# Lead stage of a decay-attention and two-layer MLP kernel: score and bonus matmuls over 128 keys, dummy matmuls of 512 columns, two groups of dummies more

## The chip, the cores and the metric

The kernel runs on one core of a Trainium2 chip. The metric is the device time of one execution in microseconds (us), and less is better. A core has five engines with a queue of instructions each: TensorE (PE in the rows, its weight loads PEld), VectorE (DVE), ScalarE (ACT), GpSimd (POOL) and SyncE (SP), which here issues the DMAs. An engine works through its queue in order; between engines, semaphores make one wait for another's result.

## The reference

An attention with a decaying state for 4 batches, 8 heads, 768 steps and 48 dimensions per head, and behind it two layers with a hidden width of 2048 over the 3072 tokens of width 384.

```python
for t in range(S):
    cur = einsum('bhd,bhe->bhde', u * k_t, v_t)           # the bonus: this step's own key and value
    y[:, :, t] = einsum('bhd,bhde->bhe', r_t, state + cur)
    state = w * state + einsum('bhd,bhe->bhde', k_t, v_t)  # w decays the state
x = y as 3072 x 384
x = relu(x @ moe_w_in) ** 2 @ moe_w_out
h = x @ moe2_w_in;  out = (h - tanh(h)) @ moe2_w_out
```

## The kernel before

**Tiling.** The 768 steps are cut into 6 chunks of 128 (`C`), so there are 24 tiles of 128 tokens (`NTAU`), four (`TPB`) for each block of 512 tokens (`TB`); block 0 holds the first chunk of all four batches. The two layers work on 6 blocks with 16 column groups of the hidden width each. Their matmuls are 128x512 in fp32r, with two-part operands, so that one column group takes 9 matmuls into the hidden layer and 9 out of it.

**The lead stage.** The first chunk of each batch has no state before it. So tiles 0 to 3 are done by functions of their own, `lead_*`, and this is what the change touches. For tile i: `lead_prod` (DVE) multiplies r and k for the bonus; `lead_k` and `lead_r` (DVE) put the decay into k and r; `lead_sums` (PE, L567, tile `pk`) sums the product over the dimensions, weighted with u, and gives one number for each key and head; `lead_bt` (ACT, L578) copies these to SBUF, `lead_diag` (POOL, L351) sets them on the diagonal of a score tile `am`; `lead_turn` (PE, L574) transposes k, `lead_kn` (ACT, L584) copies that out; `lead_b` (PE, L602, tile `sc`) computes the scores of 4 heads, `lead_m` (DVE, L613) copies them into `am` below the diagonal; `lead_c` (PE, L636, tile `y`) multiplies the scores with the values; `lead_cs` and `lead_st` (PE L650, ACT L668) compute the state; `lead_eh` and `lead_el` (ACT L659, DVE L663) give the block's input `xt` for the first layer. Besides, `table_keys` (DVE, L281, tile `kh`) and `table_turn` (PE, L291) make a table of decays that later tiles use.

**fp32 and array tiles.** These small matmuls are in plain fp32, and the trace shows each as two records, with two weight loads; a transpose has one. A matmul is given a part of the 128x128 array by where its operands lie: r and k of the two heads of a pair lie on partitions 0 to 47 and 64 to 111, and the keys of a tile are cut into two halves `c` of 64 (`L`), so the four matmuls of a head pair in `lead_b` take the four quarters of the array.

**Dummies.** `fill(n)` issues n bf16 matmuls with zero weights into a bank whose result nobody reads. 28 (`WARM`) stand ahead of everything, and `fl` in the order below issues 4 more at a time.

**Order.** The order on every engine is written out by hand in `first_order`, a list of names with an index, from which `make` calls the functions; `pb` is `lead_sums`, `tp` `lead_turn`, `lb` `lead_b` (two of them for each tile), `lm` `lead_m`, `lc` `lead_cs`, `ly` `lead_c`, `lst` `lead_st`, `tt` `table_turn`, `fl` `fill`, `h` a column group of the first layer, `c0` to `c3` the steps that unpack a weight tile `raw` (`c1a` is DVE's L96). From `h.0` on the blocks of the two layers follow each other to the end.

Of the kernel before, what the change touches and what calls it, by code (L numbers as in the profile page):

```python
# [8 lines left out]
BF16 = mybir.dt.bfloat16  # L9
# [16 lines left out]
def decay_attention_moe_moe_kernel(  # L26
# [10 lines left out]
    nc = tc.nc  # L37
    NTAU, _, _, NP, C = rk.shape
# [3 lines left out]
    GP = 64 + D  # L42
# [3 lines left out]
    TB = 512  # L46
    NB = NT // TB
    TPB = TB // C
    WARM = 28

    wts = ctx.enter_context(tc.tile_pool(name="wts", bufs=1))
    ident = wts.tile([128, 128], F32, name="ident")
    zero = wts.tile([GP, 128], BF16, name="zero")
# [10 lines left out]
    def bank(i, name):  # L64
        return ps.tile([128, 512], F32, tag=f"bank{i}", name=name)
# [7 lines left out]
    def load_w(layer, f):  # L73
        raw = cv.tile([128, 2 * DM, 2], U32, tag="raw", name="raw", bufs=5)
        nc.sync.dma_start(
            out=raw.rearrange("p x two -> p (x two)"), in_=(w1 if layer == 1 else w2).bitcast(U32)[f]
        )
        raw_t[layer, f] = raw
# [60 lines left out]
    L = C // 2  # L139
# [10 lines left out]
    low = ac.tile([128, 128], F32, name="low")  # L150
    ub = ac.tile([128, GPS], F32, name="ub")
# [3 lines left out]
    tk = tr[:, :, 127::-1]  # L155
# [8 lines left out]
    ucol = wu[:, NP:3 * NP].rearrange("p (P a) -> p P a", a=2)  # L164
# [9 lines left out]
    def hold():  # L174
        nc.gpsimd.tensor_copy(turn[0:made[0].shape[0]], made[0])

    rk_t = {}
# [11 lines left out]
    pr_t = {}  # L189
# [78 lines left out]
    def side():  # L268
        if not side_t:
            side_t.append(bank(2, "pt"))  # L270
        return side_t[0]
# [7 lines left out]
    def table_keys():  # L279
        kh = gp.tile([GP, NP, L], F32, tag="g", name="kh")  # L280
        nc.vector.tensor_tensor(  # L281
            kh, pw[:, 0, :, 63::-1], pw[:, 0, :, 32:33].to_broadcast([GP, NP, L]), op=ALU.mult,
        )
        kh_t.append(kh)

    def table_turn():
        kh_t.append(side())
        for p in range(NP):
            for a in range(2):
                q = slice(64 * a, 64 * a + D)  # L290
                nc.tensor.matmul(  # L291
                    kh_t[1][half(a), p * D:(p + 1) * D], lhsT=kh_t[0][q, p, :], rhs=ident[q, q],
                    start=True, stop=True,
                )

    def table_nat():
        nc.scalar.activation(out=kt_tab, in_=kh_t[1][:, 0:GPS], func=AF.Copy)

    def fill(n):
        for q in range(n):  # L300
            nc.tensor.matmul(
                side()[:, 256:512], lhsT=zero, rhs=low[0:GP].bitcast(BF16), start=True, stop=True
            )

    def setup_pool():
# [40 lines left out]
    def half(a):  # L346
        return slice(64 * (1 - a), 64 * (2 - a))
# [215 lines left out]
    def lead_sums(i):  # L563
        pk = pk_t[i] = bank(1, "pk")
        for p in range(NP):
            for c in range(2):
                nc.tensor.matmul(  # L567
                    pk[64 * c:64 * c + 64, NP * GP + 2 * p:NP * GP + 2 * p + 2],
                    lhsT=pr_t[i][:, p, c * L:(c + 1) * L], rhs=ucol[:, p, :], start=True, stop=True,
                )  # L570

    def lead_turn(i):
        for p in range(NP):
# [20 lines left out]
    def lead_b(d):  # L594
        i, e = divmod(d, 2)
        b0 = 3 if d % 2 else 5
        sc0[d] = sc = [bank(b0 + a, "sc") for a in range(2)]
        for z in range(2):
            for a in range(2):
                s = slice(64 * a, 64 * a + D)  # L600
                for c in range(2):
                    nc.tensor.matmul(  # L602
                        sc[a][64 * c:64 * c + 64, z * C:(z + 1) * C],
                        lhsT=rk_t[i][s, 1, 2 * e + z, c * L:(c + 1) * L], rhs=rk_t[i][s, 0, 2 * e + z, :],
                        start=True, stop=True,
                    )

    am_b = []

# [12 lines left out]
    def lead_z():  # L622
        for d in range(4):
            am_b.append(gp.tile([128, 4, C], F32, tag="ghi", name="am", bufs=4))
# [270 lines left out]
    for j in range(1, NB - 1):  # L895
        for f, o in visit.items():
            i = TPB * (j + 1) + o
# [19 lines left out]
    def front(n):  # L917
# [4 lines left out]
            act2_flush()  # L922

    first_order = """
        pr.0 k.0 fl.2 fl.0 r.0 pb.0 tp.0 rk.1 rk.2 pr.2 k.2 v.1 v.0 fl.1 tk.0 gt.5 kn.0 tt.0 pr.1 v.2 tn.0 r.1 k.1
        ub.0 lbt.0 lb.0 lb.1 pb.1 lbt.1 w.0 c1a.0 dg.0 lm.0 tp.1 lc.0 rk.3 lm.1 lb.2 dg.1 lm.2 kn.1 lst.0 ly.0 r.2
        lc.1 v.3 lst.1 lb.3 pr.3 k.3 pb.2 lm.3 lb.4 lx.0 lxl.0 lbt.2 dg.2 r.3 gt.19 c0.0 tp.2 kn.2 pb.3 lc.2 w.2 c0.2
        w.1 lbt.3 c0.1 ly.1 lx.1 dg.3 gt.3 lb.5 L.4 nu.4 c1b.0 c2.0 c1a.1 lm.4 lm.5 tp.3 lxl.1 lb.6 lm.6 w.4 w.3 lb.7
        lm.7 L.5 c3.0 kn.3 c1b.1 lst.2 lc.3 ly.2 ly.3 lst.3 fl.3 lx.2 lxl.2 lx.3 lxl.3 h.0 nr.4 c1a.2 c2.1 c1b.2 c0.4
        c3.1 h.1 c1a.4 rl.0 c2.2 c3.2 sq.0 w.5 w.7 w.6 c1a.3 c0.3 c1b.3 hi.0 rl.1 gt.14 sq.1 hi.1 c2.3 c1b.4 c0.5 ar.5  # L930
        rd.5 lo.0 h.2 rl.2 sq.2 gt.4 c3.3 g2.0 g2.1 g2l.0 gt.1 w.8 c1a.5 c1b.5 h.3 ar.4 rd.4 c2.4 c3.4 w.9 h.4 hi.2
        lo.1 lo.2 c2.5 c3.5 g2.2 c1a.6 c1a.8 c0.7 rl.3 h.5 sq.3 hi.3 lo.3 c0.6 w.10 c1a.7 gt.2 c1b.7 g2.3 gt.10 ak.4
        ns.4 c1b.6 nk.4 c0.8 c1b.8 rl.4 sq.4 hi.4 g2l.2 g2.4 g2l.1 c2.7 c2.6 c3.7 rl.5 c3.6 nu.5 b.4 gt.6 c2.8 lo.4
        sq.5 c1a.10 hi.5 lo.5 c0.10 gt.9 nr.5 d.4 c3.8 gt.11 s0p.4 gt.18 sv.4 L.6 s1a.4 s1d.4 c1a.9 c0.9 c1b.10 ns.5
        ak.5 gt.8 w.12 h.7 h.6 rl.6 rl.7 sq.6 w.11 w.13 g2l.3 g2.5 hi.6 sq.7 hi.7 c1b.9 c2.9 nu.6 h.8 g2l.4 m.4 g2.6
        lo.6 lo.7 g2.7 g2l.5 g2l.6 c2.10 c0.11 c3.9 h.9 nk.5 c1a.11 rl.8 nr.6 c1b.11 sv.5 gt.0 sq.8 w.14 ns.6 s1p.4
        s1a.5 nk.6 d.5 ak.6 s0p.6 c3.10 w.15 c0.12 y.4 hi.8 rl.9 c1a.13 c2.11 c3.11 lo.8 c1a.12 c1b.12 b.5 L.7 gt.13
        sq.9 c1a.14 s0p.5 g2.8 c0.14 d.6 h.10 xh.4 xl.4 rl.10 sq.10 s1d.5 h.11 hi.10 hi.9 lo.9 ar.6 g2l.7 g2.10 c2.12
        c3.12 s1p.5 h.12 rl.11 sq.11 m.5 hi.11 lo.10 c0.13 c1b.13 rl.12 g2.9 g2l.8 sq.12 hi.12 sv.6 s1a.6 c2.13 s1p.6
        y.5 c1b.14 c2.14 xh.5 nu.7 nr.7 nk.7 ak.7 c0.15 rd.6 b.6 s1d.6 L.8 c3.13 g2.11 g2.12 gt.17 g2l.10 c1a.15 g2l.9  # L940
        c3.14 h.13 h.14 ar.7 c1b.15 c2.15 lo.11 lo.12 g2l.11 gt.15 rl.13 sq.13 nu.8 nr.8 c3.15 rl.14 sq.14 h.15 hi.14
        hi.13 m.6 s0p.7 xl.5 sv.7 y.6 gt.7 ns.7 ns.8 d.7 s1a.7 s1p.7 rd.7 b.7 L.9 lo.13 rl.15 lo.14 xh.6 gt.12 ak.8
        s1d.7 xl.6 ar.8 g2.13 g2.14 sq.15 hi.15 lo.15 g2l.12 g2l.13 gt.16 g2l.14 g2c.15 g2b.15 nk.8 m.7 y.7 xh.7 xl.7
        ar.9 ak.9 sv.8 b.8 s1a.8 nu.9 nr.9 ns.9 d.9 g2a.15 L.10 ev.1 ev.0 ev.2 h.16 h.17 s0p.8 rl.16 sq.16 hi.16 rl.17
        sq.17 hi.17 s1d.8 s1p.8 d.8 nk.9 m.8
    """
    G, V = nc.gpsimd, nc.vector

    def load_u():
        for a in range(2):  # L950
            nc.sync.dma_start(out=ub[half(a)], in_=u[:, a * GPS:(a + 1) * GPS].to_broadcast([64, GPS]))

    make = {
        "rk": first, "v": first_value, "L": load, "w": lambda f: load_w(1, f), "ub": lambda i: load_u(),
        "fl": lambda i: fill(4), "gt": lambda i: hold(), "tk": lambda i: table_keys(), "tt": lambda i: table_turn(),
        "tn": lambda i: table_nat(),
        "pr": lead_prod, "k": lead_k, "r": lead_r, "pb": lead_sums, "tp": lead_turn, "lbt": lead_bt,
        "kn": lead_kn, "dg": lead_diag, "lb": lead_b, "lm": lead_m, "ly": lead_c,
        "lc": lead_cs, "lx": lead_eh, "lxl": lead_el, "lst": lead_st,
        "c0": lambda f: conv0(1, f), "c1a": lambda f: conv1_shift(1, f), "c1b": lambda f: conv1_join(1, f),  # L960
# [20 lines left out]
    with tc.manual_schedule():  # L981
# [4 lines left out]
        warm_act()  # L986
        nc.vector.memset(pw[:, :, :, 0:1], 1.0)
        fill(WARM)
        lead_z()
        first_values()  # L990
# [171 lines left out]
```

## Time and profile before

| | |
|---|---|
| median of the runs shown | 868.85 us |
| lowest of them | 866.46 us |
| the profiled execution | 866.38 us |
| its span, first to last instruction | 864.6 us |
| PE busy, share of the span | 856.0 us, 99% |
| mean granted TensorE clock | 0.996 |

The profiled execution took 866.38 us, of which 864.6 us lie between its first and its last instruction. In the rows below, times are us from the start of the span, unless marked ns. "PEclk" is the TensorE clock that was granted, as a share of the full clock: 1.00 is 2.4 GHz and 0.50 is 1.2 GHz. The ends of matmuls are modelled in the trace, so a PE that is shown busy need not work at its full pace.

### The profile page before, as it was taken

The numbers are of one execution on the slowest core, as the hardware profiler recorded it, in microseconds if no ns is written. First come the engines' busy times: TensorE is split into PE (matmuls) and PEld (weight loads), VectorE is DVE, ScalarE is ACT, GpSimd is POOL, SyncE is SP. The second block draws the span as 40 slices with busy tenths as digits, with TensorE's granted clock in tenths as the row PEclk, the third lists the DMA queues.
The fourth block names the chain that finished last, engine by engine and source line by source line (L and its number), as shares of the span: only waits on it lengthen the run. The fifth ranks groups of instructions, "written<-read, shape, count | busy, mean of one in ns | idle before, by whom it ended". The sixth has DMA issues, their size and how long they took to land.

```text
span 864.6 us, 16203 instructions
## 1 busy us (share of the span) xinstructions
PE 856.0 (99%) x6415; PEld 703.1 (81%) x6415; DVE 616.2 (71%) x1101; ACT 639.6 (74%) x1172; POOL 216.5 (25%) x235
## 2 busy tenths in 40 slices
PE   8999999999999999999999999999999999999998
PEld 6788888888888888888888788888888888888886
DVE  6999842504332340515786999999999999999997
ACT  3889575545555555556887988988988988988996
POOL 4342555545554653531010010010010010010000
PEclk8999999999999999999999999999999999999999
DMA  9874331303212220603640100200200200200100
GB/s 315 279 241 154 119 128 55 108 37 104 59 55 91 71 93 37 237 2 110 206 160 13 61 0 1 74 1 0 74 1 1 73 1 1 74 0 1 38 1 36
DMA packets 26539, 67.20 MB, mean 78 GB/s; under 512 B 3424, under 2 KB 12000, under 8 KB 26464
## 3 DMA queue, kind: packets, MB, share of 16 engines
q1 hardware_dynamic: 26176, 65.79, 22.6%
q8 instruction: 50, 0.82, 0.4%
q10 hardware_dynamic: 288, 0.39, 0.1%
q14 instruction: 25, 0.20, 0.1%
HBM read 55.94 MB, written 9.44 MB: 76 GB/s over the span
## 4 chain that ended last, share of the span: by engine, by line
PE 97%; DMA 1%; ACT 1%; DVE 1%; issue 0%; SPq 0%; DVEq 0%; ACTq 0%
PE h L687 45%; PE acc L736 23%; PE o L860 22%; PE y L513 2%; PE sp L432 1%; PE sp L447 1%; DMA first<-in_rk_dram 1%; PE sc L602 1%; PE y L636 1%; PE pt L650 0%; PE pk L567 0%; PE pk L574 0%; ACT x2s L757 0%; DVE hy L799 0%; ACT y L797 0%
## 5 line engine op out<-in xcount | busy, mean ns | idle before, releaser
L687 PE MATMUL h<-xs,w 128*128 128x512 f32 x864 | 211.3, 389 | 0.0
L687 PE MATMUL h<-xt,w 128*128 128x512 f32 x864 | 210.4, 389 | 0.1
L687 PEld LDWEIGHTS h<-xs,w 128*128 128x128 f32 x864 | 162.2, 188 | 34.0
L687 PEld LDWEIGHTS h<-xt,w 128*128 128x128 f32 x864 | 162.0, 188 | 34.0 <-ACT xt L659 0.3
L702 ACT ACTIVATE g<-h 128x512 f32<-128x512 f32 x96 | 57.3, 598 | 130.4 <-PE h L687 99.7
L736 PE MATMUL acc<-ghi,w 128*128 128x512 f32 x576 | 150.2, 394 | 0.0
L860 PE MATMUL o<-ghi,w 128*128 128x512 f32 x574 | 148.1, 390 | 0.0
L860 PEld LDWEIGHTS o<-ghi,w 128*128 128x128 f32 x574 | 107.3, 188 | 23.3 <-ACT ob L884 1.3
L736 PEld LDWEIGHTS acc<-ghi,w 128*128 128x128 f32 x576 | 106.5, 188 | 22.9 <-ACT ghi L710 0.4
L713 POOL TENSOR_TENSOR glo<-g,ghi 128x512 fp32r<-128x512 f32 x64 | 82.6, 1291 | 140.9 <-PE acc L736 78.2
L530 DVE TENSOR_TENSOR xt<-y,xt 128x384 fp32r<-128x384 f32 x20 | 11.1, 557 | 146.9 <-ACT xt L524 146.9
L778 POOL TENSOR_TENSOR xs<-x2f,xs 128x512 fp32r<-128x512 f32 x18 | 24.4, 1357 | 358.3 <-DVE xs L777 358.3
L800 ACT ACTIVATE th<-h 128x512 f32<-128x512 f32 x96 | 57.6, 600 | 41.0 <-DVE hy L799 41.0
L860 PE MATMUL o<-glo,w 128*128 128x512 f32 x287 | 83.3, 392 | 0.3 <-DVE glo L830 0.3
L736 PE MATMUL acc<-glo,w 128*128 128x512 f32 x288 | 82.2, 389 | 0.0
L813 DVE SCALAR_TENSOR_TENSOR hy<-q,hy 128x512 f32<-128x512 f32 x96 | 76.7, 799 | 0.1
L799 DVE SCALAR_TENSOR_TENSOR hy<-h,y 128x512 f32<-128x512 f32 x96 | 65.9, 687 | 14.1 <-ACT y L797 14.0
L818 DVE COPY_PREDICATED hy<-mask,th 128x512 f32<-128x512 uint8 x96 | 70.8, 738 | 0.1
L803 DVE TENSOR_TENSOR th<-h,th 128x512 f32<-128x512 f32 x96 | 66.2, 690 | 6.1 <-ACT th L800 0.7
L801 ACT ACTIVATE q<-y,ba 128x512 f32<-128x512 f32 x96 | 68.6, 714 | 0.0
L804 ACT ACTIVATE q<-y,bb 128x512 f32<-128x512 f32 x96 | 68.5, 713 | 0.0
L807 ACT ACTIVATE mask<-y,bm 128x512 uint8<-128x512 f32 x96 | 68.3, 711 | 0.0
(114 smaller groups left out, 1114.5 us busy)
## 6 DMA issues: line engine op xcount, KB each, us to landing
raw<-in_w_dram SPq DMA_DIRECT2D x32, 768.0 KB, 5.1
rkt<-in_rk_dram SPq DMA_DIRECT2D x20, 512.0 KB, 3.8
x2d<-x2s SPq DMA_DIRECT2D x18, 256.0 KB, 2.3
x2f<-x2d SPq DMA_DIRECT2D x18, 256.0 KB, 3.4
vs<-in_nat_dram SPq DMA_DIRECT2D x40, 112.0 KB, 4.1
out_dram<-ob SPq DMA_DIRECT2D x17, 256.0 KB, 2.4
rnt<-in_nat_dram SPq DMA_DIRECT2D x20, 192.0 KB, 4.2
kn<-in_nat_dram SPq DMA_DIRECT2D x20, 192.0 KB, 4.4
```

The costliest lines, as they stand in the source:

```text
L687: nc.tensor.matmul(h, lhsT=w_in(layer, f, part, kk), rhs=x[:, xpart, kk, :], start=(n == 0), stop=(n == 3 * KK - 1),)
L713: nc.gpsimd.tensor_tensor(lo, g, hi.bitcast(F32), op=ALU.subtract)
L736: nc.tensor.matmul(acc[j][m], lhsT=w_out(1, f, part, m * 128, (m + 1) * 128), rhs=g, start=(f == 0 and n == 0), stop=(f == NF - 1 and n == 2),
L799: nc.vector.scalar_tensor_tensor(out=hy, in0=h, scalar=PK, in1=y, op0=ALU.mult, op1=ALU.mult)
L800: nc.scalar.activation(out=th, in_=h, func=AF.Tanh)
L801: nc.scalar.activation(out=q1, in_=y, func=AF.Square, bias=p2["ba"], scale=1.0)
L803: nc.vector.tensor_tensor(th, h, th, op=ALU.subtract)
L804: nc.scalar.activation(out=q2, in_=y, func=AF.Square, bias=p2["bb"], scale=1.0)
L807: nc.scalar.activation(out=mask, in_=y, func=AF.Sign, bias=p2["bm"], scale=1.0)
L813: nc.vector.scalar_tensor_tensor(out=hy, in0=q2, scalar=PD, in1=hy, op0=ALU.add, op1=ALU.mult)
L818: nc.vector.copy_predicated(hy, mask, th)
L860: nc.tensor.matmul(acc[j][m], lhsT=w, rhs=g, start=(f == 0 and n == 0), stop=n == 2 and f == (NF - 2 if m == KK - 1 and j == NB - 1 else N ...
```

## The change

Three edits, all of PE's instructions in the lead stage. The scores of a head are computed in one matmul with 128 keys as weights where there were two with 64 keys each. The bonus sums of a head pair are computed in one matmul with 128 keys as weights where there were two. A dummy has 512 columns (the same 256 read twice) and fills its whole bank, where it had 256 in half a bank; the first group has 13 where it had 28, each `fl` has 2 where it had 4, and two groups `fl.4 fl.5` are put in behind `tp.0`.

```diff
-    WARM = 28
+    WARM = 13
...
             nc.tensor.matmul(
-                side()[:, 256:512], lhsT=zero, rhs=low[0:GP].bitcast(BF16), start=True, stop=True
+                side(), lhsT=zero, rhs=low[0:GP].bitcast(BF16)[:, None, :].to_broadcast([GP, 2, 256]),
+                start=True, stop=True,
             )
...
         for p in range(NP):
-            for c in range(2):
-                nc.tensor.matmul(
-                    pk[64 * c:64 * c + 64, NP * GP + 2 * p:NP * GP + 2 * p + 2],
-                    lhsT=pr_t[i][:, p, c * L:(c + 1) * L], rhs=ucol[:, p, :], start=True, stop=True,
-                )
+            nc.tensor.matmul(
+                pk[:, NP * GP + 2 * p:NP * GP + 2 * p + 2], lhsT=pr_t[i][:, p, :], rhs=ucol[:, p, :],
+                start=True, stop=True,
+            )
...
                 s = slice(64 * a, 64 * a + D)
-                for c in range(2):
-                    nc.tensor.matmul(
-                        sc[a][64 * c:64 * c + 64, z * C:(z + 1) * C],
-                        lhsT=rk_t[i][s, 1, 2 * e + z, c * L:(c + 1) * L], rhs=rk_t[i][s, 0, 2 * e + z, :],
-                        start=True, stop=True,
-                    )
+                nc.tensor.matmul(
+                    sc[a][:, z * C:(z + 1) * C], lhsT=rk_t[i][s, 1, 2 * e + z, :], rhs=rk_t[i][s, 0, 2 * e + z, :],
+                    start=True, stop=True,
+                )
...
-        pr.0 k.0 fl.2 fl.0 r.0 pb.0 tp.0 rk.1 rk.2 pr.2 k.2 v.1 v.0 fl.1 tk.0 gt.5 kn.0 tt.0 pr.1 v.2 tn.0 r.1 k.1
+        pr.0 k.0 fl.2 fl.0 r.0 pb.0 tp.0 fl.4 fl.5 rk.1 rk.2 pr.2 k.2 v.1 v.0 fl.1 tk.0 gt.5 kn.0 tt.0 pr.1 v.2 tn.0
...
-        "fl": lambda i: fill(4), "gt": lambda i: hold(), "tk": lambda i: table_keys(), "tt": lambda i: table_turn(),
+        "fl": lambda i: fill(2), "gt": lambda i: hold(), "tk": lambda i: table_keys(), "tt": lambda i: table_turn(),
```

The rest of the list stands as it stood, and the other engines' instructions are the same in the same order.

On PE, from the first tile's sums (`pk<-wu,first`) over its transposes to the table's turn (`kh`) and the first scores, there stands before (the pair of rows for a dummy comes four times):

```order
L567 MATMUL pk<-wu,first 64x2 x8
L574 MATMUL pk<-ident,first 128x112 x4
L301 LDWEIGHTS zero
L301 MATMUL pt<-low,zero 128x256
...
L291 MATMUL pt<-ident,kh 64x48 x8
L602 MATMUL sc<-first 64x128 x16
```

And now, where the pair of rows for a dummy comes six times:

```order
L567 MATMUL pk<-wu,first 128x2 x4
L574 MATMUL pk<-ident,first 128x112 x4
L301 LDWEIGHTS zero
L301 MATMUL pt<-low,zero 128x512
...
L291 MATMUL pt<-ident,kh 64x48 x8
L601 MATMUL sc<-first 128x128 x8
```

Between the transposes and the table's turn stand 6 dummies of 512 columns in place of 4 of 256, and the sums ahead of them are half as many, each over 128 keys.

On PE, from the second tile's sums to the first `y` and the next tile's state, there stands before:

```order
L567 MATMUL pk<-wu,first 64x2 x8
L574 MATMUL pk<-ident,first 128x112 x4
L650 MATMUL pt<-first_v,first_kn 64x48 x8
L602 MATMUL sc<-first 64x128 x8
L636 MATMUL y<-am,first_v 32x128 x16
L650 MATMUL pt<-first_v,first_kn 48x48 x8
```

And now:

```order
L567 MATMUL pk<-wu,first 128x2 x4
L574 MATMUL pk<-ident,first 128x112 x4
L648 MATMUL pt<-first_v,first_kn 64x48 x8
L601 MATMUL sc<-first 128x128 x4
L634 MATMUL y<-am,first_v 32x128 x16
L648 MATMUL pt<-first_v,first_kn 48x48 x8
```

Nothing has moved against its neighbours here; sums and scores are half as many and twice as wide in weights, and all else is as it was.

## Rows read from the trace of the kernel before

**Rows 1.** The page: busy time of the engines, chain of waits by engine

```profile
PE 856.0 (99%) x6415; PEld 703.1 (81%) x6415; DVE 616.2 (71%) x1101; ACT 639.6 (74%) x1172; POOL 216.5 (25%) x235
...
PE 97%; DMA 1%; ACT 1%; DVE 1%; issue 0%; SPq 0%; DVEq 0%; ACTq 0%
```

**Rows 2.** Stretches: busy time of each engine, granted clock, DMA

```profile
core 0: us, PE busy (x) PEld busy (x) DVE busy (x) ACT busy (x) POOL busy (x), PEclk, DMA share, GB/s
8.79:10.72 1.93, 0.00 (x0) 0.00 (x1) 1.77 (x4) 0.14 (x1) 0.31 (x1) 1.00 1.10 415
...
11.70:18.54 6.84, 6.56 (x105) 5.25 (x97) 4.68 (x11) 1.73 (x8) 2.99 (x4) 0.50 1.01 387
...
30.00:100.00 70.00, 69.98 (x719) 57.27 (x720) 66.63 (x127) 60.61 (x111) 26.82 (x32) 1.00 0.58 192
```

**Rows 3.** The chain that ended last: start, duration, what

```profile
8.84 0.70 DVE first L539
...
10.33 0.35 DVE kh L281
...
17.03 1.75 PE y L636 x32
...
19.27 0.60 PE sc L602 x16
19.87 0.56 PE pk L567 x16
...
21.03 0.55 PE pk L574 x4
...
23.23 1.01 PE y L636 x32
...
45.34 2.04 PE h L687 x9
```

**Rows 4.** PE in order of time: start, duration, what [idle before, releaser]

```profile
8.19 0.60 PE L301 MATMUL pt<-low,zero 112*128 112x256 bf16 x4
10.72 0.49 PE L291 MATMUL pt<-ident,kh 48*64 48x48 f32 x10 [1.93 <-DVE kh L281]
...
16.96 1.82 PE L636 MATMUL y<-am,first_v 128*32 128x128 f32 x32
18.71 0.56 PE L650 MATMUL pt<-first_v,first_kn 128*48 128x48 f32 x16
...
22.20 0.63 PE L567 MATMUL pk<-wu,first 112*64 112x2 f32 x16 [0.63 <-ACT first_kn L584]
```

**Rows 5.** DVE and the end of the lead in order of time

```profile
13.05 1.04 DVE L96 TENSOR_SCALAR raw<-raw 128x768 uint32<-128x768 uint32 x1 [0.46 <-DMA raw<-in_w_dram]
14.01 1.42 DVE L613 COPY_PREDICATED am<-low,sc 128x256 f32<-128x256 uint32 x4
17.13 0.78 DVE L613 COPY_PREDICATED am<-low,sc 128x256 f32<-128x256 uint32 x2 [1.70 <-PE sc L602]
27.54 0.88 ACT L668 ACTIVATE st<-pt,wst 112x48 f32<-112x48 f32 x4 [0.71 <-PE pt L650]
29.31 0.61 PE L301 MATMUL pt<-low,zero 112*128 112x256 bf16 x4
```

**Rows 6.** Weight loads by line and form, 18.6 to 42: busy us, mean ns

```profile
L687 PEld LDWEIGHTS h<-xt,w 128*128 128x128 f32 x38 | 7.1, 188 | 1.8 <-ACT xt L659 0.3
L636 PEld LDWEIGHTS y<-am,first_v 128*32 128x32 f32 x64 | 1.6, 109 | 0.1
L567 PEld LDWEIGHTS pk<-wu,first 112*64 112x64 f32 x32 | 1.1, 137 | 1.0 <-ACT first_kn L584 0.8 <-issue 0.2
L574 PEld LDWEIGHTS pk<-ident,first 112*128 112x128 f32 x8 | 0.8, 140 | 0.3 <-ACT bt L578 0.2 <-issue 0.2
```

**Rows 7.** Dummies of PE, 18.6 to 42 by form, and before 4.8 in time

```profile
L301 PE MATMUL pt<-low,zero 112*128 112x256 bf16 x4 | 0.6, 275 | 0.0
...
1.56 3.51 PE L301 MATMUL pt<-low,zero 112*128 112x256 bf16 x16 [1.56 <-POOL low L308]
```

More of the change, by code (lines that the diff above doesn't have):

```diff
@@ L924, in decay_attention_moe_moe_kernel @@
     first_order = """
-        pr.0 k.0 fl.2 fl.0 r.0 pb.0 tp.0 rk.1 rk.2 pr.2 k.2 v.1 v.0 fl.1 tk.0 gt.5 kn.0 tt.0 pr.1 v.2 tn.0 r.1 k.1
[L926 to L944, printed above, removed]
@@ L945, in decay_attention_moe_moe_kernel @@
-        sq.17 hi.17 s1d.8 s1p.8 d.8 nk.9 m.8
+        pr.0 k.0 fl.2 fl.0 r.0 pb.0 tp.0 fl.4 fl.5 rk.1 rk.2 pr.2 k.2 v.1 v.0 fl.1 tk.0 gt.5 kn.0 tt.0 pr.1 v.2 tn.0
+        r.1 k.1 ub.0 lbt.0 lb.0 lb.1 pb.1 lbt.1 w.0 c1a.0 dg.0 lm.0 tp.1 lc.0 rk.3 lm.1 lb.2 dg.1 lm.2 kn.1 lst.0 ly.0
+        r.2 lc.1 v.3 lst.1 lb.3 pr.3 k.3 pb.2 lm.3 lb.4 lx.0 lxl.0 lbt.2 dg.2 r.3 gt.19 c0.0 tp.2 kn.2 pb.3 lc.2 w.2
+        c0.2 w.1 lbt.3 c0.1 ly.1 lx.1 dg.3 gt.3 lb.5 L.4 nu.4 c1b.0 c2.0 c1a.1 lm.4 lm.5 tp.3 lxl.1 lb.6 lm.6 w.4 w.3
@@ new lines, in decay_attention_moe_moe_kernel @@
+        lb.7 lm.7 L.5 c3.0 kn.3 c1b.1 lst.2 lc.3 ly.2 ly.3 lst.3 fl.3 lx.2 lxl.2 lx.3 lxl.3 h.0 nr.4 c1a.2 c2.1 c1b.2
+        c0.4 c3.1 h.1 c1a.4 rl.0 c2.2 c3.2 sq.0 w.5 w.7 w.6 c1a.3 c0.3 c1b.3 hi.0 rl.1 gt.14 sq.1 hi.1 c2.3 c1b.4 c0.5
+        ar.5 rd.5 lo.0 h.2 rl.2 sq.2 gt.4 c3.3 g2.0 g2.1 g2l.0 gt.1 w.8 c1a.5 c1b.5 h.3 ar.4 rd.4 c2.4 c3.4 w.9 h.4
+        hi.2 lo.1 lo.2 c2.5 c3.5 g2.2 c1a.6 c1a.8 c0.7 rl.3 h.5 sq.3 hi.3 lo.3 c0.6 w.10 c1a.7 gt.2 c1b.7 g2.3 gt.10
+        ak.4 ns.4 c1b.6 nk.4 c0.8 c1b.8 rl.4 sq.4 hi.4 g2l.2 g2.4 g2l.1 c2.7 c2.6 c3.7 rl.5 c3.6 nu.5 b.4 gt.6 c2.8
@@ new lines, in decay_attention_moe_moe_kernel @@
+        lo.4 sq.5 c1a.10 hi.5 lo.5 c0.10 gt.9 nr.5 d.4 c3.8 gt.11 s0p.4 gt.18 sv.4 L.6 s1a.4 s1d.4 c1a.9 c0.9 c1b.10
+        ns.5 ak.5 gt.8 w.12 h.7 h.6 rl.6 rl.7 sq.6 w.11 w.13 g2l.3 g2.5 hi.6 sq.7 hi.7 c1b.9 c2.9 nu.6 h.8 g2l.4 m.4
+        g2.6 lo.6 lo.7 g2.7 g2l.5 g2l.6 c2.10 c0.11 c3.9 h.9 nk.5 c1a.11 rl.8 nr.6 c1b.11 sv.5 gt.0 sq.8 w.14 ns.6
+        s1p.4 s1a.5 nk.6 d.5 ak.6 s0p.6 c3.10 w.15 c0.12 y.4 hi.8 rl.9 c1a.13 c2.11 c3.11 lo.8 c1a.12 c1b.12 b.5 L.7
+        gt.13 sq.9 c1a.14 s0p.5 g2.8 c0.14 d.6 h.10 xh.4 xl.4 rl.10 sq.10 s1d.5 h.11 hi.10 hi.9 lo.9 ar.6 g2l.7 g2.10
@@ new lines, in decay_attention_moe_moe_kernel @@
+        c2.12 c3.12 s1p.5 h.12 rl.11 sq.11 m.5 hi.11 lo.10 c0.13 c1b.13 rl.12 g2.9 g2l.8 sq.12 hi.12 sv.6 s1a.6 c2.13
+        s1p.6 y.5 c1b.14 c2.14 xh.5 nu.7 nr.7 nk.7 ak.7 c0.15 rd.6 b.6 s1d.6 L.8 c3.13 g2.11 g2.12 gt.17 g2l.10 c1a.15
+        g2l.9 c3.14 h.13 h.14 ar.7 c1b.15 c2.15 lo.11 lo.12 g2l.11 gt.15 rl.13 sq.13 nu.8 nr.8 c3.15 rl.14 sq.14 h.15
+        hi.14 hi.13 m.6 s0p.7 xl.5 sv.7 y.6 gt.7 ns.7 ns.8 d.7 s1a.7 s1p.7 rd.7 b.7 L.9 lo.13 rl.15 lo.14 xh.6 gt.12
+        ak.8 s1d.7 xl.6 ar.8 g2.13 g2.14 sq.15 hi.15 lo.15 g2l.12 g2l.13 gt.16 g2l.14 g2c.15 g2b.15 nk.8 m.7 y.7 xh.7
@@ L946, in decay_attention_moe_moe_kernel @@
+        xl.7 ar.9 ak.9 sv.8 b.8 s1a.8 nu.9 nr.9 ns.9 d.9 g2a.15 L.10 ev.1 ev.0 ev.2 h.16 h.17 s0p.8 rl.16 sq.16 hi.16
+        rl.17 sq.17 hi.17 s1d.8 s1p.8 d.8 nk.9 m.8
     """
```

## The prediction

> **What bounds the kernel now.** I read the page first: PE is busy for 99% of the span, and 97% of the chain that ended last is PE's [rows 1]. The reader is to see that time can only come from two places, work of PE that goes away and the few microseconds in which PE waits or runs slowly. The table of stretches then says where these are. From 30 us on PE is busy 69.98 of 70 us at the full clock [rows 2], and so to the end; the matmuls there are not touched. So the change can only move the moment at which the first layer's matmuls begin, and whatever it moves there comes out at the end, as long as the other engines keep up. The lead stage before 30 us has two weak places. PE stands idle for 1.93 us, from 8.79 to 10.72 [rows 2, 4], since the chain runs there through DVE: the product of tile 1 at 8.84, r times decay, then `kh` at 10.33, which the table's turn on PE waits for [rows 3]. And in the stretch from 11.70 to 18.54 the granted clock is 0.50, that is 1.2 GHz, although PE is busy 6.56 of 6.84 us in it [rows 2]. Before the fall PE had been idle for 1.93 us; a wait of 0.63 us at 21.6 to 22.2 was followed by no fall [rows 4]. From 10.72 on, PE is the chain.
>
> **The dummies.** At the full clock four dummies of 256 take 0.60 us and one of them 275 ns [rows 4, 7], so they follow each other at (0.60 - 0.275) / 3 = 0.108 us, and a dummy of 512 should take 0.216. At the start they run at half of that: 16 of them take 3.51 us, 0.22 each [rows 7], which is the pace of 1.2 GHz. Ahead of the first sums stand 17 of 512 columns (34 times 256) where 36 of 256 stood, so these end some 0.2 us earlier. Behind the transposes stand 6 x 0.216 = 1.30 us where 4 x 0.108 = 0.43 stood: 0.87 more. None of this is on the path, for the table's turn waits for `kh` at 10.68 either way, and the idle 1.93 us is the cover. With the first sums 0.4 us longer (next part) the wait shrinks to 1.93 - 0.87 - 0.4 + 0.2 = 0.9 to 1.2 us, by whether the gap before the sums goes too. If the cover were gone, each 0.1 us over would be lost in full. The last group, `fl.3`, keeps its 1024 columns. Its dummies now write the whole bank that the last state copies read, so they wait for these too; the copies end at 27.54 + 0.88 = 28.42 and the group begins at 29.31 [rows 5], so 0.9 us of other work covers that.
>
> A rule of the Trainium skill can be held against this price. The page "TensorE: Matmul & The Clock Gate", section "Back-to-back issue gap", gives about 131 ns for each matmul of 512 columns in a stream of loads and matmuls, while 9 of them take 2.04 us here, 227 ns each [rows 3], so the trace disagrees. By that rule six dummies would be over in about 0.8 us (an estimate from that page), PE's wait would stay near 1.5 us, and the clock's fall would be the likelier outcome.
>
> **What the clock is worth.** If the clock stays at 1.00, I follow the chain from 10.72 with rows at the full clock: table's turn 0.49 [rows 4]; scores of tile 0, two groups of 0.60 [rows 3] and 0.15 for the change of array tiles and a longer first load, to 12.55; sums 0.56 [rows 3] + 0.4, to 13.5; the copy to SBUF and back to PE, 0.25; transposes 0.55 [rows 3], to 14.3; state 0.5 [rows 4], scores 0.65, so `y` could begin at about 15.55. The masks it needs come from DVE, which sits on a weight tile's landing until 13.05 and ends the four L613 at 14.01 + 1.42 = 15.43 [rows 5]; that doesn't depend on PE and leaves PE the later one by a hair. Before, `y` began at 16.96 [rows 4]. So 1.4 us come back there. The 32 records of `y` took 1.75 us in the chain at the low clock and 1.01 at the full one [rows 3]: 0.74. Together 2.1 us, and the tile's next state begins at about 16.6, not 18.71 [rows 4]. DVE follows, since its own wait of 1.70 us before L613 at 17.13 was for these scores [rows 5].
>
> **The sums.** Eight fp32 matmuls (16 records in pairs, the pair side by side in the two column halves) become four over all 128 columns, 8 records one after the other. They multiply 2 columns, so the load sets the pace. What a load of 128 fp32 columns costs here no row shows. From below: a transpose's load of 128 takes 140 ns, hardly more than the 137 of the sums' 64; then nothing is lost. From above: the fp32r loads of 128 columns take 188 [rows 6], 51 ns more than 137, and the line through 109 for 32 columns and 137 for 64 gives 193. A transpose has one pass, the sums two, so I take the upper price: 8 x 51 ns = 0.41 us a tile. Tile 0's sums lie before the wait, tile 1's are in the 15.55 above, and those of tiles 2 and 3, at 19.87 [rows 3] and at 22.20 [rows 4], are in the chain: + 0.8 us.
>
> **The scores.** Four quarters of the array at a time become two halves. The streaming is the same: four rounds in a group's 0.60 us [rows 3], 0.15 each with the gaps. By the line above a load of 128 has 128 x 0.875 ns = 0.11 us of its own, so it still fits behind the matmul before it; only the first load of a group can't hide and is 0.05 us longer, in the four groups that stand behind `y` (tile 3's two count as one): + 0.2 us. From below this is nothing, and if no load hid, a group would be 4 x 0.05 longer: those ends are 0.2 us and 0.8 us.
>
> **The sum.** - 2.1 + 0.8 + 0.2 = - 1.1 us, against the profiled execution's 866.4: **865.3 us**. That execution lies at the lowest of the runs shown (866.46), the median is 868.85, so another execution can lie 2.4 us off by itself; I set my forecast beside the former.
>
> **The rivals.**
>
> *The clock falls all the same, and the kernel is slower.* The place is the same as before, some 1 us after the table's turn. For it: a wait of about 1.1 us stays, sums that stream two columns are now longer, and PE still waits for the copy behind them. Against it: the wait is halved, and after 0.63 us it didn't fall. It decides itself by whether 1.1 us is on the side of 0.63 or of 1.93. Then the 2.1 us don't come back, tile 1's sums, at half the clock, cost 0.85 on the path, and the 1.0 of later sums and scores stays: 866.4 + 1.9 = 868.3. Where it falls later, in the sums of tile 1 or behind, and as long, some 0.5 us more: 868.8.
>
> *The clock rises late.* Dummies run at the half pace until about 4.9 us here. If it rose only behind the first 17, they end at 1.56 + 17 x 0.43 = 8.9, sums and transposes at half the clock 2.9, to 11.8, six dummies 1.3, to 13.1: the table's turn comes 2.4 us late: 867.7. For it: six dummies are more than the cover then; against it: the one trace that there is.
>
> *The weight loads are free,* as the 140 ns have it: the 0.8 and 0.2 are not lost, 864.3.
>
> *The weight loads hide behind nothing.* Each of the sums' 8 records would wait for load and matmul; a pair takes 0.56 / 8 = 0.07 now, at most that much more a record, 2 x 8 x 0.07 = 1.1: 866.4. Against it: dummies of the same rows follow at 0.108, the time of 256 columns at 2.4 GHz. The Trainium skill, "TensorE: Matmul & The Clock Gate", Part 3, section "The mechanism", says that a weight load overlaps with a running matmul only when their row groups differ; the sums' don't, and by that rule this would happen, but the dummies' pace disagrees.
>
> *DVE becomes the bound.* It is busy 66.63 of 70 us behind the lead [rows 2]. If it can't follow, the 1.1 us are lost there: 866.4. Against it: in the lead it waits for PE, so it comes earlier as well.
>
> **How the numbers follow.** Clock stays, loads at the upper price: 0.50 (865.3; own range 864.3 to 866.0). Clock falls: 0.25 (868.3 to 868.8). Late rise 0.10, loads free 0.07, nothing hides 0.03, DVE 0.05. From 864.0 to 868.9 all of these are held; what is left out are falls that last longer and executions that differ by themselves. Within 2% means within 17 us, about what a measurement of this kernel can tell from no change, and no case here reaches that: within 2% 0.98, faster and slower 0.01 each.
>
> **What would show it.** Granted clock 1.00 from 4.9 us to the end; PE's wait before the table's turn 0.9 to 1.2 us; `y` of tile 0 at 15.4 to 15.7; 8 records of sums in about 1 us, with loads near 190 ns; score groups of 0.6 to 0.7; the first layer's first matmul at 28.9, where it was at 30.0. I am wrong if the granted clock is 0.50 in any stretch between 10 and 860 us, or if the first layer begins 1 us earlier and the end doesn't.

## The result and the profile after

The change made the kernel slower: 872.32 us in the median where the kernel before has 867.81, a ratio of 1.0051 (95% interval 1.0036 to 1.0066). Like every difference between medians in this document, that is within 2%. Measured once more (`e16_after_again`) it was 872.03 against 866.36, a ratio of 1.0073 (1.0058 to 1.0088). The ratios are those on record and can differ by some 0.001 from the quotient of two medians. Forecast were 865.3 us, in a range from 864.0 to 868.9. The profiled execution took 872.23 us with a span of 870.5, 5.9 longer than before.

One thing is needed to read every number below: executions of one and the same kernel differ in how long the granted clock is 0.50, which in the profiled ones is in the lead stage, and each result lists the mean granted clock of every execution. (This mean takes the clock as 1.00 until it is first recorded, so the slow start isn't in it.) Of the kernel before, 133 executions in four comparisons have that number: 11 with 1.000 took 864.9 us in the mean, 44 with 0.998 took 865.5, 42 with 0.994 took 867.6, 4 with 0.988 took 871.4. Its profile on which the forecast rests (0.996) lies in the middle. Of the changed kernel's 20 executions 4 had 0.998 (866.9 us) and 16 had 0.992 or less (870.5 to 875.1). So at one and the same mean clock of 0.998 the change costs 1.4 us; the rest of the loss goes with the clock. One execution of the kernel before (2204.24 us) and one of `e8` (1437.11 us) lie far above all others and are left out of the ratios and mean clocks, though not out of the medians (868.48 for `e8`, 868.21 without it).

The stretches of the changed kernel, with the same columns as [rows 2]; the granted clock stands behind POOL's busy time:

```profile
1.57:7.04 5.47, 5.47 (x13) 1.87 (x13) 3.67 (x13) 1.89 (x4) 4.82 (x19) 1.00 0.83 251
...
10.76:13.87 3.11, 2.84 (x41) 2.58 (x42) 2.77 (x6) 0.58 (x3) 1.92 (x2) 1.00 1.00 407
13.87:20.70 6.83, 6.83 (x85) 5.44 (x85) 3.67 (x9) 2.47 (x10) 1.35 (x3) 0.50 1.04 392
20.70:24.11 3.41, 2.78 (x27) 2.43 (x26) 3.04 (x6) 2.36 (x5) 2.01 (x2) 1.00 1.01 356
24.11:34.35 10.24, 10.24 (x133) 8.72 (x136) 5.95 (x12) 4.65 (x14) 4.12 (x7) 0.50 0.42 146
34.35:100.00 65.65, 65.57 (x613) 53.37 (x606) 62.32 (x112) 56.66 (x100) 23.91 (x29) 1.00 0.58 198
```

The first row shows 1.00 because no clock is recorded ahead of the rise at 7.04; its 13 dummies took 5.47 us, 0.42 each, which is half the pace of the full clock. Then the clock fell twice, for 6.83 and for 10.24 us, where [rows 2] have one stretch of 6.84. The first fall is as long as before and comes 2.2 us later, as the rise does (7.04 and 4.88). In both falls PE is busy all the time. From 34.35 on PE is busy 65.57 of 65.65 us, as before.

PE in order of time, with the columns of [rows 4]:

```profile
1.57 6.52 PE L301 MATMUL pt<-low,zero 112*128 112x512 bf16 x17 [1.57 <-POOL low L309]
...
9.15 1.46 PE L301 MATMUL pt<-low,zero 112*128 112x512 bf16 x6
10.76 0.67 PE L291 MATMUL pt<-ident,kh 48*64 48x48 f32 x16 [0.15 <-DVE kh L281]
...
12.45 1.05 PE L567 MATMUL pk<-wu,first 112*128 112x2 f32 x8
13.77 0.97 PE L574 MATMUL pk<-ident,first 112*128 112x112 f32 x4 [0.27 <-ACT bt L578]
...
16.85 1.93 PE L634 MATMUL y<-am,first_v 128*32 128x128 f32 x32
18.72 0.88 PE L648 MATMUL pt<-first_v,first_kn 128*48 128x48 f32 x16
...
20.69 1.05 PE L567 MATMUL pk<-wu,first 112*128 112x2 f32 x8
21.67 0.72 PE L601 MATMUL sc<-first 48*128 48x128 f32 x8
...
23.55 1.39 PE L567 MATMUL pk<-wu,first 112*128 112x2 f32 x8 [0.63 <-ACT first_kn L584]
...
35.93 6.42 PE L685 MATMUL h<-xt,w 128*128 128x512 f32 x27
```

Three things are to be seen. PE waited only 0.15 us before the table's turn, where it had waited 1.93 [rows 4], and the clock fell all the same: not behind that wait but at 13.87, behind the sums of tile 1, which end at 13.5. Up to the state of tile 1 nothing is won or lost: 18.72 where [rows 4] have 18.71, for `y` ran at the half clock again. And the first layer begins at 35.93, not at 29.98, 5.95 us later, which is the whole difference of the spans. So all that was lost was lost between 18.7 and 35.9.

The chain of the changed kernel there, start, duration and what, as in [rows 3]:

```profile
18.79 0.81 PE pt L648 x16
19.60 1.16 PE sc L601 x8
20.76 0.98 PE pk L567 x8
21.74 0.65 PE sc L601 x8
...
23.55 1.39 PE pk L567 x8
24.94 0.81 PE pt L648 x16
25.75 1.87 PE y L634 x32
27.62 1.16 PE sc L601 x8
28.78 0.94 PE pk L574 x4
29.71 2.01 PE sc L601 x16
31.72 0.81 PE pt L648 x16
32.53 2.83 PE y L634 x64
```

And pieces of the chain of before that [rows 3] leave out:

```profile
18.78 0.49 PE pt L650 x16
...
22.20 0.63 PE pk L567 x16
22.83 0.40 PE pt L650 x16
...
27.49 1.93 PE y L636 x64
```

Against these, the two pieces ahead of 20.7, still in the first fall, cost 0.9 us more: 0.81 for 0.49, and the scores took 1.16 where [rows 3] have 0.60. The sums at 20.76 ran at the full clock and took 0.98 where [rows 3] have 0.56: 0.42, and the scores behind them 0.05 more. The sums of tile 3 took 1.39 for 0.63: 0.42 again and some 0.35 through the second fall, which caught their end. From 24.94 to 34.35 all pieces are in the second fall; `y` took 1.87 where [rows 3] have 1.01, and the way from 24.94 to 35.36 took 10.42 us where before it took 6.59 (22.83 to 29.42): 3.8 more. So of 5.95 us some 0.9 are the wider loads and some 5.1 the clock.

### The profile page after: what moved, and what is told of

It reads as the page before. It is cut to its first block, busy times and chain, and to the rows that moved or that the text cites. A ratio compares the mean times of both kernels' runs of the same rounds, so it can differ in the third digit from the quotient of the medians.

```text
span 870.5 us, 15973 instructions
## 1 busy us (share of the span) xinstructions
PE 863.8 (99%) x6300; PEld 707.3 (81%) x6300; DVE 616.7 (71%) x1101; ACT 640.3 (74%) x1172; POOL 215.8 (25%) x235
## 4 chain that ended last, share of the span: by engine, by line
PE 97%; DMA 1%; ACT 1%; DVE 1%; issue 0%; SPq 0%; DVEq 0%; ACTq 0%
PE h L685 45%; PE acc L734 23%; PE o L858 22%; PE y L514 2%; PE sp L433 1%; PE sp L448 1%; PE sc L601 1%; DMA first<-in_rk_dram 1%; PE y L634 1%; PE pt L648 0%; PE pk L567 0%; PE pk L574 0%; ACT x2s L755 0%; DVE hy L797 0%; ACT y L795 0%
```

## The experiments

All of them are the kernel before or the changed kernel with single parts exchanged. Every ratio is to the kernel before, run on the same chip. "Mean clock" is the mean of the granted clock over the executions; the kernel before has 0.995 to 0.996 in all four comparisons, the changed kernel 0.991 in both.

Three theories went in, and rivals named with each run: A, the wide sums cost their loads and, as matmuls of two columns that now take longer, let the clock fall a second time; B, the dummies' edit does it; C, the scores' loads of 128 columns do it.

**One part alone.** `e1_dummies` has only the dummies' edit (512 columns each instead of 256):

```diff
-    WARM = 28
+    WARM = 13
-        "fl": lambda i: fill(4), ...
+        "fl": lambda i: fill(2), ...
-        ... pb.0 tp.0 rk.1 ...
+        ... pb.0 tp.0 fl.4 fl.5 rk.1 ...
```

> The dummies' edit alone (13 + 6 x 2 of 512 columns, two groups more); sums and scores as before. Theory A (the wide sums are what costs: 0.42 us a tile, and a longer stretch in which TensorE streams two columns, after which the granted clock falls a second time): no second fall, so the same as the kernel before or up to 2 us less, median 865.5 to 868. Theory B (the denser dummies and their place bring the second fall): slower like the whole change, about 872.

Measured: 866.65 us, ratio 1.0004 (0.9988 to 1.0020), mean clock 0.9966. The dummies alone gain or lose nothing that can be told from none; B falls.

`e2_scores` has only the scores' edit:

```diff
-                for c in range(2):
-                    nc.tensor.matmul(sc[a][64 * c:64 * c + 64, ...], lhsT=rk_t[i][s, 1, 2 * e + z, c * L:(c + 1) * L], ...)
+                nc.tensor.matmul(sc[a][:, ...], lhsT=rk_t[i][s, 1, 2 * e + z, :], ...)
```

> The scores' edit alone (one matmul per head over 128 keys). Theories A and B: within 1 us of the kernel before, 867 to 869, one stretch at half the clock. Theory C (loads of 128 columns in two row halves no longer hide, and stretch all score groups): 1 to 4 us slower, 869 to 872.

Measured: 866.19 us, ratio 1.0007 (0.9985 to 1.0028), mean clock 0.9946; so C isn't the cause of the loss. Yet 3 of its 12 executions took 871 to 873 us with a clock of 0.986 to 0.990, and the profiled one has two falls, so the scores' edit may have a small part in the falls, and two falls also come with sums over 64 keys.

`e3_sums` has only the sums' edit:

```diff
-            for c in range(2):
-                nc.tensor.matmul(pk[64 * c:64 * c + 64, ...], lhsT=pr_t[i][:, p, c * L:(c + 1) * L], ...)
+            nc.tensor.matmul(pk[:, ...], lhsT=pr_t[i][:, p, :], ...)
```

> The sums' edit alone (one matmul per head pair over 128 keys). Theory A: slower by the loads, 2 x 0.4 us, and in many executions by a second fall of the clock, median 869.5 to 873. Theories B and C: at most 1 us slower, 868 to 869.

Measured: 867.96 us, ratio 1.0020 (1.0002 to 1.0038), mean clock 0.9947. Slower, as A wants it, but by 1.5 us only and so below its range: the sums alone are not the whole loss.

**One part undone.** `e4_no_sums` is the changed kernel with the sums over 64 keys as before.

> The whole change with the sums undone (dummies and scores of the change, sums over 64 keys as before). Theory A: the loss is gone, 865.5 to 868.5. Theory B or C: it stays, 870 to 873.

Measured: 864.67 us, ratio 0.9969 (0.9955 to 0.9984), mean clock 0.9989; none of its 10 executions is below 0.998. The kernel before has 866.46 in the same comparison, so this version is faster than both kernels, by 1.8 us in the medians here. `e11_no_sums_again` is the same kernel, measured again with the experiments further below:

> The whole change with the sums undone, once more, beside the two kernels that add to it and on their chip. If the first result holds: 864 to 866, some 2 us faster than the kernel before, mean granted clock 0.998 or more.

864.94 us, ratio 0.9985 (0.9970 to 1.0000), mean clock 0.9977: the gain is there again, smaller and at the edge of its interval, with 4 of 12 executions at 0.994 to 0.996. The first profile shows what the forecast had hoped for. Its busy times by stretch, with the columns of [rows 2]:

```profile
7.83:27.76 19.93, 18.63 (x363) 14.34 (x361) 17.47 (x35) 11.59 (x34) 9.02 (x14) 1.00 1.04 375
```

One stretch from the clock's rise to the end of the lead stage, at the full clock, and in order of time:

```profile
12.49 0.63 PE L568 MATMUL pk<-wu,first 112*64 112x2 f32 x16
...
15.18 1.08 PE L635 MATMUL y<-am,first_v 128*32 128x128 f32 x32
...
17.33 0.63 PE L568 MATMUL pk<-wu,first 112*64 112x2 f32 x16
17.89 0.71 PE L602 MATMUL sc<-first 48*128 48x128 f32 x8
...
27.76 4.42 PE L686 MATMUL h<-xt,w 128*128 128x512 f32 x18
```

The first layer begins at 27.76 instead of 29.98, and the span is 862.2 instead of 864.6: what comes back in the lead stage comes out at the end.

`e5_no_scores` is the changed kernel with the scores of before, `e6_no_dummies` with the dummies of before.

> The whole change with the scores undone (dummies and sums of the change, scores over 64 keys as before). Theory A (the wide sums alone bring the loads' 0.8 us and the second fall of the clock; the scores' edit plays no part): 870 to 873 like the whole change. Rival E (it takes sums and scores together to make the clock fall twice): 866 to 868, mean granted clock 0.994 or more in most runs.

> Sums and scores of the change, dummies as before. Theory A: 868 to 872, since the dummies lie ahead of the first sums and only shift when the clock rises first. Rival F (the changed dummies are what makes the wide sums so harmful): as the sums alone, 867.5 to 868.5.

Measured: 869.65 us without the scores' edit, ratio 1.0016 (0.9992 to 1.0041), mean clock 0.9938, half of the executions at 0.992 or below; and 872.21 without the dummies' edit, ratio 1.0047 (1.0025 to 1.0069), mean clock 0.9915, as the whole change. So the loss doesn't need the dummies' edit (rival F falls), sums and scores together have all of it, and the sums with the scores of before some part, so that both A and rival E are only half right.

**Few columns or more time.** These kernels put work in behind the sums of tiles 1, 2 and 3. `e8_no_sums_thin` adds to `e4` 14 bf16 matmuls of 2 columns each time, `e9_no_sums_thick` four dummies of 256, both meant to be some 0.4 us; `e7_after_thick` adds the same four dummies of 256 to the whole change. In the edit `fx` issues `fill_thin` in `e8` and `fill_half` in the other two.

```diff
-        ... pb.1 lbt.1 ... pb.2 lm.3 ... pb.3 lc.2 ...
+        ... pb.1 fx.1 lbt.1 ... pb.2 fx.2 lm.3 ... pb.3 fx.3 lc.2 ...
+    def fill_thin(n):
+        ...
+        nc.tensor.matmul(side()[:, 256:258], lhsT=zero, rhs=low[0:GP, 0:1].bitcast(BF16), ...)
+    def fill_half(n):
+        ...
+        nc.tensor.matmul(side()[:, 256:512], lhsT=zero, rhs=low[0:GP].bitcast(BF16), ...)
```

> Dummies and scores of the change, sums over 64 keys as before, and behind the sums of tiles 1, 2 and 3 14 bf16 matmuls of 2 columns, some 0.4 us each time, as much as the wide sums took longer. Theory A: the clock falls again as in the whole change, mean granted clock 0.994 or less in most runs, 868 to 872. Rival H (the fp32 loads of 128 columns themselves, not the missing columns, bring the falls): the clock stays at 0.998 or more, 865 to 866, the added time alone.

> Dummies and scores of the change, sums over 64 keys, and behind the sums of tiles 1, 2 and 3 four dummies of 256 columns (0.43 us each time): the same added time as the 14 matmuls of 2 columns of the experiment before, but with many columns. Theory A (missing columns let the clock fall): mean granted clock 0.998 or more, 865 to 866, the added time alone. Rival I (any added time behind the sums shifts the lead stage so that the clock falls): 868 or more, mean clock 0.995 or less.

> The whole change with four dummies of 256 columns in half a bank (0.43 us at the full clock) put in behind the sums of tiles 1, 2 and 3. TensorE has up to 1.3 us more to do. Theory A (it is the long stretch of two-column matmuls that lets the clock fall): the clock stays up more often, mean granted clock 0.996 or more, 866 to 868.5, so faster than the whole change in spite of the added work. Rival G (the time lost in the lead is simply work, and more work makes it worse): 873 or more.

Measured: with matmuls of 2 columns 868.48 us, ratio 1.0016 (0.9992 to 1.0039), mean clock 0.9941; with 256 columns 865.81 us, ratio 0.9998 (0.9983 to 1.0014), mean clock 0.9983. The profile of the thin one has the same two falls as the whole change, though its sums have loads of 64 columns; its busy times by stretch:

```profile
13.42:20.25 6.83, 6.83 (x100) 5.66 (x98) 4.54 (x10) 2.12 (x9) 2.21 (x4) 0.50 1.03 385
20.25:23.66 3.41, 2.78 (x56) 2.29 (x56) 2.94 (x6) 2.55 (x7) 2.11 (x2) 1.00 1.03 346
23.66:33.90 10.24, 10.24 (x152) 8.72 (x154) 5.37 (x12) 4.96 (x14) 4.32 (x7) 0.50 0.47 171
```

and its order of time around each fall:

```profile
12.87 0.63 PE L574 MATMUL pk<-wu,first 112*64 112x2 f32 x16
13.44 0.53 PE L308 MATMUL pt<-low,zero 112*128 112x2 bf16 x14
...
23.43 0.85 PE L574 MATMUL pk<-wu,first 112*64 112x2 f32 x16 [0.63 <-ACT first_kn L591]
24.21 0.53 PE L308 MATMUL pt<-low,zero 112*128 112x2 bf16 x14
```

The falls at 13.42 and 23.66 come while the sums run, whose matmuls have two columns, but just ahead of the thin matmuls of the same tile (13.44 and 24.21), so in this execution the first fall can't be their work. What is left is how often it happens: 4 of 11 executions of `e8` have a mean clock of 0.992 or less, none of 22 of `e4` and `e11`, and 1 of 12 of `e9`. This speaks against the loads of 128 columns as the only cause (rival H) and against added time (rival I), as the same time with many columns leaves the clock nearly as it was in `e4` and costs 0.9 to 1.1 us. It doesn't prove it: the two were compared on different chips, and the intervals of their ratios overlap. The whole change with the dummies of 256 columns has 869.84 us, ratio 1.0025 (1.0005 to 1.0045), mean clock 0.9952: up to 1.3 us more work and some 2 us less time than the whole change, so the loss is not simply work (rival G). Time and clock miss what A expected (868.5 and 0.996); the added dummies are on the path.

**In PE's waits alone.** `e10_no_sums_idle` and `e12_dummies_idle` put two dummies of 256 behind tile 1's sums and four ahead of tile 3's, where PE waits for ScalarE, into `e4` and into `e1`; `e15_after_idle` puts the four ahead of tile 3's sums into the whole change.

```diff
-        ... pb.1 lbt.1 ... kn.2 pb.3 ...
+        ... pb.1 fx.2 lbt.1 ... kn.2 fx.4 pb.3 ...
+        "fx": lambda i: fill_half(i),
```

> Dummies and scores of the change, sums over 64 keys, and dummies of 256 columns only where TensorE waits anyway: two behind the sums of tile 1, four ahead of the sums of tile 3. Theory A: the best of all, 864 to 865, mean granted clock 0.999 or more. Rival I: 865 to 868.

> The dummies of the change, sums and scores as before, and the dummies of 256 columns in TensorE's two waits. The dummies alone left the clock at 0.9966 in the mean, with the scores' edit at 0.9989. If the scores' edit helps because it fills the array better over the same time, dummies in the waits can do the same: mean clock 0.998 or more, 864.5 to 866. If it helps in another way: 866 to 868, mean clock 0.997 or less.

> The whole change with four dummies of 256 columns in TensorE's wait of 0.63 us ahead of the sums of tile 3, so at next to no time of their own. Theory A: the second fall becomes rarer, mean clock 0.994 or more, 867 to 870.5. If this wait plays no part: as the whole change, 872.

Measured: `e10` 864.46 us, the lowest median of all, with 9 of 12 executions at 0.999 or 1.000; but two at 872 and 873 us, a mean clock of 0.9973, below the 0.999 that A expected, and a ratio of 0.9994 (0.9971 to 1.0018). The profiled execution is one of these two. Its busy times by stretch:

```profile
4.81:11.64 6.83, 5.36 (x54) 3.02 (x54) 5.03 (x12) 1.35 (x4) 2.95 (x12) 1.00 0.97 334
11.64:35.53 23.89, 23.89 (x290) 19.72 (x292) 14.72 (x29) 9.91 (x30) 9.13 (x12) 0.50 0.76 262
```

and PE in order of time, with the columns of [rows 4]:

```profile
10.84 0.67 PE L291 MATMUL pt<-ident,kh 48*64 48x48 f32 x16 [1.47 <-DVE kh L281]
```

Here the clock rose early (4.81), the dummies were over early, PE waited 1.47 us before the table's turn, and the clock fell at 11.64 and stayed down for 23.89 us. That looks like the wait's work, but the profile of `e12` has the same early rise (5.09) and the same wait, and the clock stayed up for 20.48 us:

```profile
5.09:25.57 20.48, 16.77 (x340) 11.95 (x338) 16.31 (x34) 10.43 (x29) 11.77 (x23) 1.00 0.99 374
...
10.98 0.49 PE L291 MATMUL pt<-ident,kh 48*64 48x48 f32 x10 [1.48 <-DVE kh L281]
```

So a wait of nearly 1.5 us before the table's turn was followed by a fall in one execution and by none in another. `e12` has 866.20 us, ratio 0.9997 (0.9982 to 1.0012), mean clock 0.9988: the dummies in the waits lift the clock as the scores' edit does, but the time stays that of the kernel before. In its profile PE stood still for 2.09 us from 23.53 with no releaser shown, and the clock fell at 25.57; whether its other executions lose their time in the same way no profile shows. `e15` has 869.23 us, ratio 1.0026 (1.0001 to 1.0050), mean clock 0.9950, as A expected: 6 of 12 executions are at 0.992 or less, of the whole change 22 of 27. Its profiled execution (865.29 us) kept the clock from 5.93 us to the last 0.9 us of its span, and so shows the whole change as the forecast had it:

```profile
5.93:28.80 22.87, 21.31 (x341) 16.72 (x339) 18.50 (x39) 11.73 (x35) 11.59 (x20) 1.00 1.00 359
...
15.52 1.08 PE L640 MATMUL y<-am,first_v 128*32 128x128 f32 x32
...
28.80 6.43 PE L691 MATMUL h<-xt,w 128*128 128x512 f32 x27
```

**Which sums.** `e13_wide_01` has wide sums in tiles 0 and 1 alone, `e14_wide_23` in tiles 2 and 3 alone, and `e16_after_again` is the whole change on the same chip. The edit is that of `e13`, against the changed kernel; `e14` has the condition the other way round.

```diff
-            nc.tensor.matmul(pk[:, ...], lhsT=pr_t[i][:, p, :], ...)
+            for c in range(1 if i < 2 else 2):
+                m = slice(0, C) if i < 2 else slice(c * L, (c + 1) * L)
+                nc.tensor.matmul(pk[m, ...], lhsT=pr_t[i][:, p, m], ...)
```

> The whole change with wide sums in tiles 0 and 1 alone, 64 keys in tiles 2 and 3. Theory A in its sharper form (the second fall, which costs the most, comes from the sums of tiles 2 and 3, behind the clock's first recovery): the second fall is gone, 865.5 to 868, mean granted clock 0.996 or more. Rival J (the first fall, behind tile 1's sums, decides, and the second follows from it): 870 to 873.

> The whole change with wide sums in tiles 2 and 3 alone. Theory A in its sharper form: nearly all of the loss stays, 869 to 872.5, mean granted clock 0.994 or less. Rival J: 866 to 867.5, the loads of two tiles and no more.

> The whole change once more, on the chip of the three kernels beside it. If the first measurement holds: 871 to 873, mean granted clock 0.99 to 0.993.

Measured: 866.91 us, ratio 1.0011 (0.9989 to 1.0033), mean clock 0.9953; 866.84 us, ratio 1.0020 (0.9998 to 1.0041), mean clock 0.9958; and the whole change 872.03, mean clock 0.9911. Neither half brings the loss. The sharper form of A expected it with tiles 2 and 3, rival J with tiles 0 and 1, and both fall: the whole loss takes the wide sums in both places, and the scores' edit beside them.

The profile of `e16` is one of its milder executions (867.25 us), and its stretches differ from those of the same kernel above:

```profile
5.85:19.50 13.65, 13.01 (x170) 10.07 (x168) 11.59 (x26) 5.34 (x18) 6.40 (x14) 1.00 1.03 396
19.50:26.33 6.83, 6.57 (x68) 5.49 (x69) 2.77 (x7) 3.29 (x6) 3.82 (x6) 0.50 1.02 369
```

The clock rose earlier, at 5.85 instead of 7.04, stayed up past the wide sums of tiles 1 and 2 and fell once, at 19.50, in PE's wait ahead of tile 3's sums. So the order of PE's instructions alone doesn't fix where the clock falls.

**Counted by executions.** At a mean clock of 0.992 or less are 14 of 133 executions of the kernel before, 1 of 12 of `e1`, 3 of 12 of `e2`, 4 of 12 of `e3`, none of 22 of `e4` and `e11`, 6 of 12 of `e5`, 9 of 12 of `e6`, 1 of 12 of `e7`, 2 and 3 of 12 of `e13` and `e14`, and 22 of 27 of the changed kernel. So the wide sums make long falls frequent, most of all beside the scores' edit, and without them they are rarer.

## Why the prediction was wrong

**What bounds the kernel: right.** The difference of the first layer's begin (5.95 us later in the change, 2.2 earlier in `e4`) comes out in the span (5.9 and 2.4), and VectorE didn't hold `e4` back; the rival on DVE is out.

**The dummies: pace right, place wrong.** Six of 512 columns took 1.46 us with the last one's tail, as reckoned at 0.216 each. But the step "a wait of 0.9 to 1.2 us stays" took the clock's rise at 4.88 us from one execution. It rose at 7.04 in the profile after, so the first 17 ended at 8.1 and PE's wait was 0.15 us. The late rise, a rival with a chance of 0.10, thus happened in a milder form, 2.2 us late and not the 4 us that it was priced with, and the table's turn began at 10.76 all the same.

**The loads: right.** A load of the wide sums takes 193 ns, as the line through 32 and 64 columns had it. The weight loads of the changed kernel from 20.7 to 24 us, grouped by line and form (busy us and mean ns of one behind the first bar):

```profile
L567 PEld LDWEIGHTS pk<-wu,first 112*128 112x128 f32 x13 | 1.6, 193 | 1.1 <-ACT first_kn L584 0.8 <-issue 0.2
L574 PEld LDWEIGHTS pk<-ident,first 112*128 112x128 f32 x4 | 0.4, 140 | 0.1
```

The sums of a tile cost 0.42 us more (forecast 0.41), a group of scores 0.05 more (0.72 for 0.67). The rivals "loads are free" and "loads hide behind nothing" are out.

**What the clock is worth: right.** The profile of `e15`, the whole change with four dummies in a wait of PE, kept its clock. It has `y` at 15.52 (forecast 15.55), the first layer at 28.80 (28.9) and took 865.29 us (865.3). `e4`, without the 0.4 us of wide sums ahead of `y`, has it at 15.18. So with the clock up the whole sum comes out, and only its condition failed.

**That the clock stays: wrong, and this is the step that failed.** It was put as "before the fall PE had been idle for 1.93 us", and the chance of 0.50 was drawn from how far the dummies would shorten that wait. The runs show that the length of the wait doesn't decide it. In the profile after, the wait was 0.15 us and the clock was at 0.50 from 13.87 to 20.70, behind the sums of tile 1, whose matmuls have two columns, and from 24.11 to 34.35, while and after those of tile 3 ran; in `e12` a wait of 1.48 us was followed by no fall there. The edit to the sums, which was priced at 0.8 us by its loads, had a second price that the sum doesn't hold: with it undone (`e4`, `e11`) no execution of 22 is at 0.992 or less, with it 22 of 27. Why it has this price is argued and not shown: it makes the stretches of two-column matmuls longer, and `e7`, `e8` and `e9` speak for that, for added matmuls of 256 columns raised the mean clock beside the wide sums (0.9952 for 0.991) and left it nearly alone beside the narrow ones (0.9983), where those of 2 columns lowered it (0.9941). The rival that the clock falls all the same was priced with one fall of the length before (868.3 to 868.8); it was given 0.25 and came, in the profile, with two falls and 5.1 us. The condition by which it was to decide itself, a wait nearer to 0.63 or to 1.93 us, is the same failed step.

**What stays open.** Why one and the same kernel has its falls at 13.87 and 24.11 in one execution and at 19.50 in another. Why the whole loss comes only when all the sums are wide and the scores' edit is there too (`e3`, `e5`, `e13`, `e14` against `e6` and the whole change), and why the scores' edit alone lowers the mean clock slightly (0.9946) but raises it beside the dummies (0.9989 and 0.9977 in `e4` and `e11`, 0.9966 in `e1`). The executions vary enough that 12 of them leave the latter two undecided.

## What to carry to other kernels

Where TensorE is the bound, read the granted clock beside its busy time, stage by stage and over several executions: one profile shows one case of it. An edit that halves the number of matmuls by doubling their weights isn't free where few columns stream behind the loads: here the sums of 2 columns took 0.98 us for 0.56, the scores of 128 columns 0.65 for 0.60. And the clock can be a second price of an edit, larger than the first; a forecast that needs the clock to stay up should price both cases over many executions. A dummy costs its time wherever PE doesn't wait, and put into the waits it brought no gain that these runs can tell from none (`e10`, `e12`).

## What the runs showed of the hardware

The clock's first rise came at 4.8 to 7.9 us in the profiled executions (4.88 before, 7.04 after, 5.85 for the same kernel in `e16`, 7.83 in `e4`, 4.81 in `e10`), with dummies from 1.6 us on in all of them. A TensorE that hardly waits can lose its clock: in the 3.11 us ahead of the first fall of the changed kernel PE was busy for 2.84. And an fp32 load of 128 columns, 193 ns here, is longer than that of a transpose of the same width, 140 ns.
